# Sliding-window attention and dropless mixture of experts on one core: routing by pairs of batches, x stored times its probability, a tile's last additions moved into the next

## The chip, the cores and the metric

The kernel runs on one NeuronCore of a Trainium2 chip. The metric is device time in microseconds (us) of one execution: the median of the runs, 875.6 us before the change.

The engines are named as the profile names them: PE (TensorE matmuls; PEld its weight loads), DVE (VectorE), ACT (ScalarE), POOL (GpSimd) and SP (SyncE, which only issues DMAs here). Each works through its own queue in order and waits on semaphores for the others.

## The reference

```python
B, H, S, D = 8, 8, 576, 64            # attention: window of 64 positions, causal
mask = (rel >= 0) & (rel < 64)        # rel = query position - key position
attn = softmax(where(mask, q @ k.T / sqrt(D), -1e9));  o = attn @ v
x = o.transpose(0, 2, 1, 3).reshape(4608, 512)
logits = x @ w_gate                   # 8 experts
expert = argmax(logits);  gate = softmax(logits)[expert]
y[rows of expert e] = relu(x[rows of e] @ w1[e]) @ w2[e]   # w1: 512 x 1024, w2: 1024 x 512
out = gate[:, None] * y               # 4608 x 512, f32
```

Every token goes to one expert and none is dropped. With the inputs of this case the experts get 669, 400, 748, 505, 592, 390, 566 and 738 tokens.

## The kernel before, in words

**Attention.** Work goes by 16 units: a pair of batches (`bg`, 4 of them) times a pair of heads (`g`, 4). A unit has 9 blocks of 128 query rows and is worked in three steps of three blocks, so there are 48 steps. The loop at L381 writes a software pipeline: in step `s` it issues `scored(s+1)` (mask and scores into PSUM, row maximum L282 on DVE, exp L285 on ACT), `weighted(s-1)` (probabilities times values, L309; division into `xs`, L318), `turned(s+2)` (transposes of q and k, L233, copied out by ACT L238 and DVE L240), `flipped(s)` (transposes of the probabilities, L294, copied by DVE and ACT L296) and `x_turned(s-2)` (transposes of x, L332, copied at L335). A scheduler orders this stage's instructions by the order in the source and by readiness.

**Gate logits and the store of x.** `routed(u)` multiplies the turned x by the gate's weights (L355); after the fourth pair of heads the logits of the two batches are turned back and copied into the tile `logits` (L368). `x_turned` stores finished x rows into `x_dram` by DMAs on ACT's queue (L340, L346).

**Routing.** After all of attention, on the logits of all 4608 tokens at once (36 columns of 128 tokens, 8 experts), lines L420 to L540: the maximum and a one-hot of its first place (L448 to L454), the probability `gate` (L455 to L461), counts before each token by two f32 matmuls with a triangular and a full matrix of ones (L467, L468) and a scan (L470), how many tiles each expert takes (L480 to L497), the slot of each token (L505 to L512), and one-hots of the slot's low 7 bits (`lo`, L524) and of its column (`hi`, L526), the latter also times the token's number and its probability (L529, L530). 36 matmuls (L533) add these up into `slots`; `perm_i` (L537) says which token sits in each slot, `gate_t` (L539, L540) with which probability. The routing pool `rt` and the second weights' pool `wp` lie in memory that attention's pools had; `load_w` (L138, L139) fetches w1 and w2 of an expert on SP's queue.

**Experts.** Tiles of 256 tokens, in an order written out by hand (`manual_schedule`, L551). Each product of 2x2 blocks is done with seven block products instead of eight, so sums of blocks are formed: of the weights by POOL (`sums_w1`, `sums_w2`: four additions each, L121), of x and of the hidden layer by DVE (`sums_x`, and `left_sums` into `hs`, both L121 too). `body` is one tile: `hidden` (L609 to L631), `turn` (transposes of the next tile's x, L593, L594), `gather` (indirect DMA of x rows for the tile after that, L573), `output` (L640 to L671), `scatter` (indirect DMA of result rows to `out`, L582). In `output` every read of a product multiplies by the token's probability: ACT at L655, L656, L659, DVE at L647 (`onto`). A full tile has 256 tokens; an odd last chunk of 128 is done with plain matmuls (`plain_hidden`, `plain_output`). An expert runs its first tile inside `tc.If(chunks > 1)` (L735), then the odd one inside `tc.If(odd > 0)` (L740), then the others in nested Ifs (L743 to L751). The counts give 19 full tiles and 2 odd ones (experts 4 and 6). Where an If is not taken, every engine passes a block that raises its semaphore by what the skipped instructions would have, once its own earlier work is done.

**Order on POOL's and DVE's queues.** POOL: gather of the tile after next, scatter at the tile's end (behind DVE's last addition), the copy of the next probabilities, then `sums_w1(e+1)` ahead of an expert's first tile and `sums_w2(e+1)` behind it. DVE in `output`: four sums into `hs`, four of `sums_x`, then the seven `onto`.

Of the kernel before, what the change touches and what calls it, by code (L numbers as in the profile page):

```python
# [10 lines left out]
F32 = mybir.dt.float32  # L11
BF16 = mybir.dt.bfloat16
# [23 lines left out]
def kernel(  # L36
# [47 lines left out]
    logits = consts.tile([P, E, NJ], F32, name="logits")  # L84
    perm_i = consts.tile([P, NS], I32, name="perm_i")
    gate_t = consts.tile([P, NX, C + 1], F32, name="gate_t")
# [3 lines left out]
    starts_i = consts.tile([P, E], I32, name="starts_i")  # L90
    halves_i = consts.tile([P, E], I32, name="halves_i")
    w1v = moe_w1.rearrange("e (g p) f -> p e g f", p=P)
    w2v = moe_w2.rearrange("e (t p) d -> p e t d", p=P)
    weights = lambda pool, i: [
        pool.tile([P, 1, NG, FF], F32, name=f"w1_{i}"), pool.tile([P, 1, FT, DM], F32, name=f"w2_{i}")
    ]
    ws = [weights(consts, 0)]
# [3 lines left out]
    sums_of = lambda pool, i: (  # L101
        pool.tile([P, 4, HG, HD], F32, name=f"s1_{i}"), pool.tile([P, 4, HF, HM], F32, name=f"s2_{i}")
    )
    sums = [sums_of(consts, 0)]
# [18 lines left out]
    def w1q(e):  # L123
        w = ws[e % NW][0][:, 0]
        return [w[:, a * HG : (a + 1) * HG, f * HD : (f + 1) * HD] for f in range(2) for a in range(2)]

    def w2q(e):
        w = ws[e % NW][1][:, 0]
        return [w[:, f * HF : (f + 1) * HF, a * HM : (a + 1) * HM] for f in range(2) for a in range(2)]

    def sums_w1(e):
        form(left_sums(G, sums[e % NW][0], *w1q(e)))

    def sums_w2(e):
        form(right_sums(G, sums[e % NW][1], *w2q(e)))

    def load_w(e):
        nc.sync.dma_start(out=ws[e % NW][0][:], in_=w1v[:, e : e + 1, :, :])  # L138
        nc.sync.dma_start(out=ws[e % NW][1][:], in_=w2v[:, e : e + 1, :, :])  # L139
# [12 lines left out]
    with (  # L152
# [172 lines left out]
        def x_turned(s):  # L325
# [12 lines left out]
            if g == NG - 1 and c:  # L338
                x, t0 = xss[bg], (bg * BG + c - 1) * S
                nc.scalar.dma_start(  # L340
                    out=x_dram[t0 : t0 + SM, :].rearrange("(n p) d -> p n d", p=P), in_=x[:, (c - 1) * NV : c * NV, :]
                )
                if c == NST - 1:
                    for i in range(BG):
                        t0 = (bg * BG + i) * S + SM
                        nc.scalar.dma_start(out=x_dram[t0 : t0 + D, :], in_=x[i * D : (i + 1) * D, BG * NV, :])  # L346

        WC = 32
        def routed(u):

# [8 lines left out]
            if g == NG - 1:  # L359
# [3 lines left out]
                for m in range(ST):  # L363
# [3 lines left out]
                    )  # L367
                nc.vector.tensor_copy(  # L368
                    out=logits[:, :, bg * NTB : (bg + 1) * NTB].rearrange("p e (c m) -> p e c m", c=NST),
                    in_=tr[:, :, :, 0:E].rearrange("p m c e -> p e c m"),  # L370
                )

# [8 lines left out]
        for s in range(-2, N + 4):  # L381
            if s == N - 2 * NST:
                load_w(0)
            if s == N - NST:
                sums_w1(0)
                sums_w2(0)
# [16 lines left out]
    ws.append(weights(wp, 1))  # L403
    sums.append(sums_of(wp, 1))
    load_w(1)


    with (
# [3 lines left out]
        def iota(shape, pattern, base=0, cm=0):  # L412
            t = rt.tile(shape, F32, name=f"iota{len(iotas)}")
            nc.gpsimd.iota(
                t[:], pattern=pattern, base=base, channel_multiplier=cm, allow_small_or_imprecise_dtypes=True
            )
            iotas.append(t)
            return t

        iotas = []  # L420
        e_m = iota([P, E], [[1, E]], base=-E)
        lane = iota([P, P], [[1, P]])
        hi_id = iota([P, NS], [[1, NS]], base=-C)
        cuts = iota([P, NCUT], [[P, NCUT]])

        tok_m = rt.tile([P, NJ], F32, name="tok_m")
        tok_g = tok_m[:].rearrange("p (g j) -> p g j", j=NTB)
# [352 lines left out]
```

## Time and profile before

| | |
|---|---|
| time, median of 3 runs | 875.6 us (875.54 to 877.23) |
| the profiled execution | 876.49 us |
| its span, first to last instruction | 874.8 us |
| mean granted TensorE clock | 0.959 |
| PE busy | 780.4 us (89%) |
| PEld busy | 664.8 us (76%) |
| DVE busy | 430.0 us (49%) |
| ACT busy | 237.7 us (27%) |
| POOL busy | 307.7 us (35%) |
| HBM read, written | 73.94 MB, 20.45 MB |

Busy time is the time in which an engine had an instruction of the program at work. A row of a timeline gives the start in us, the length, the engine, the line, the operation, the tiles as out<-in, the shapes, and in square brackets the idle time before it with what ended it. A row of waits gives who waited for whom, the total in us, how often, and the longest. "DVEq" and "PEq" are an engine's sequencer, such as its branch at the line named. A window's row gives busy time and number of instructions of each engine, the granted clock, the share of the DMA engines and GB/s.

### The profile page before, as it was taken

The numbers are of one execution on the slowest core, as the hardware profiler recorded it, in microseconds if no ns is written. First come the engines' busy times: TensorE is split into PE (matmuls) and PEld (weight loads), VectorE is DVE, ScalarE is ACT, GpSimd is POOL, SyncE is SP. The second block draws the span as 40 slices with busy tenths as digits, with TensorE's granted clock in tenths as the row PEclk, the third lists the DMA queues.
The fourth block names the chain that finished last, engine by engine and source line by source line (L and its number), as shares of the span: only waits on it lengthen the run. The fifth ranks groups of instructions, "written<-read, shape, count | busy, mean of one in ns | idle before, by whom it ended". The sixth has DMA issues, their size and how long they took to land. (4 is left out here: it accounts for less than half of the span.)

```text
span 874.8 us, 17497 instructions
## 1 busy us (share of the span) xinstructions
PE 780.4 (89%) x6832; PEld 664.8 (76%) x6832; DVE 430.0 (49%) x818; ACT 237.7 (27%) x606; POOL 307.7 (35%) x312
## 2 busy tenths in 40 slices
PE   7998998998981479999998999889999899999992
PEld 5775776676750478999887999779888888888992
DVE  4664665665644543444436343545444436344341
ACT  4553554553530012222111221112122111121220
POOL 3221221245000063415626522735715626621121
PEclk9998999998995689999999999999999999999997
DMA  6668667878025011015143115115215143110110
GB/s 137 152 138 232 155 155 217 216 177 245 9 89 213 0 49 50 25 50 209 50 158 111 37 49 218 49 56 191 77 31 214 49 157 113 49 45 25 50 49 23
DMA packets 140302, 94.48 MB, mean 108 GB/s; under 512 B 118032, under 2 KB 118032, under 8 KB 140178
## 3 DMA queue, kind: packets, MB, share of 16 engines
q1 hardware_dynamic: 128274, 61.90, 25.3%
q0 software_dynamic: 7040, 21.50, 7.5%
q10 hardware_dynamic: 4864, 9.44, 3.0%
q8 instruction: 75, 1.23, 0.6%
q14 instruction: 49, 0.40, 0.2%
HBM read 73.94 MB, written 20.45 MB: 108 GB/s over the span
## 5 line engine op out<-in xcount | busy, mean ns | idle before, releaser
L609 PE MATMUL hp<-xs,s 128*128 128x128 f32 x912 | 108.4, 276 | 0.5 <-DVE part L618 0.5
L640 PE MATMUL yp<-s,hs 128*128 128x256 f32 x456 | 103.4, 381 | 4.7 <-DVE hs L121 4.7
L609 PEld LDWEIGHTS hp<-xs,s 128*128 128x128 f32 x912 | 105.3, 193 | 0.7 <-DVE part L618 0.7
L640 PEld LDWEIGHTS yp<-s,hs 128*128 128x128 f32 x456 | 85.9, 190 | 19.6 <-DVE hs L121 8.3
L582 POOL DMA_INDIRECT out_dram<-y,at_s x42 | 42.5, 1011 | 163.6 <-DVEq L745 51.4
L285 ACT ACTIVATE pr<-sc,mx 128x128 f32<-128x128 f32 x288 | 79.4, 374 | 70.6 <-DVE mx L282 52.6
L121 POOL TENSOR_TENSOR s<-w 128x1024 f32<-128x1024 f32 x32 | 78.3, 2449 | 57.2 <-DMA out_dram<-y,at_s 38.3
L609 PE MATMUL hp<-xq,w 128*128 128x128 f32 x608 | 76.6, 280 | 15.4 <-DVEq L740 7.9
L609 PEld LDWEIGHTS hp<-xq,w 128*128 128x128 f32 x608 | 73.0, 196 | 21.2 <-issue 21.0
L573 POOL DMA_INDIRECT xg<-x_dram,at_g x46 | 50.3, 1094 | 79.4 <-PE tp L593 69.1
L640 PE MATMUL yp<-w,hq 128*128 128x256 f32 x304 | 71.9, 379 | 0.0
L282 DVE TENSOR_REDUCE mx<-sc 128x3 f32<-128x384 f32 x96 | 49.1, 553 | 41.8 <-PE sc L275 40.3
L216 POOL COPY vb<-va 64x520 f32<-64x520 f32 x32 | 19.7, 616 | 126.7 <-DMA va<-in_v_dram 89.5
L647 DVE SCALAR_TENSOR_TENSOR party<-yp,gates,party 128x256 f32<-128x256 f32 x76 | 34.9, 479 | 57.4 <-PE yp L640 56.2
L640 PEld LDWEIGHTS yp<-w,hq 128*128 128x128 f32 x304 | 56.3, 190 | 6.8
L616 ACT COPY part<-hp 128x512 f32<-128x512 f32 x19 | 11.1, 585 | 160.5 <-PE hp L609 160.5
L121 DVE TENSOR_TENSOR hs<-hq 128x512 f32<-128x512 f32 x38 | 45.2, 1190 | 13.2 <-ACT hq L631 13.2
L618 DVE TENSOR_TENSOR part<-hp,part 128x512 f32<-128x512 f32 x19 | 13.1, 691 | 76.3 <-PE hp L609 76.3
L294 PEld LDWEIGHTS tr<-ident,pr 128*128 128x128 f32 x288 | 34.9, 146 | 20.0 <-ACT qT L238 8.3
L294 PE MATMUL tr<-ident,pr 128*128 128x128 f32 x288 | 49.7, 288 | 0.1
L275 PE MATMUL sc<-kT,qT 64*64 64x128 f32 x1152 | 47.2, 287 | 0.1
L275 PEld LDWEIGHTS sc<-kT,qT 64*64 64x64 f32 x1152 | 33.9, 138 | 12.6 <-issue 8.6
(141 smaller groups left out, 1350.9 us busy)
## 6 DMA issues: line engine op xcount, KB each, us to landing
w<-in_moe_w_dram SPq DMA_DIRECT2D x16, 2048.0 KB, 11.3
qs<-in_q_dram SPq DMA_DIRECT2D x64, 128.0 KB, 3.2
ks<-in_k_dram SPq DMA_DIRECT2D x64, 128.0 KB, 3.1
va<-in_v_dram SPq DMA_DIRECT2D x64, 128.0 KB, 2.8
x_dram<-xs ACTq DMA_DIRECT2D x8, 1024.0 KB, 6.1
qs<-in_q_dram SPq DMA_DIRECT2D x32, 32.0 KB, 2.6
ks<-in_k_dram SPq DMA_DIRECT2D x32, 32.0 KB, 2.2
vb<-in_v_dram SPq DMA_DIRECT2D x32, 32.0 KB, 2.7
```

What stands on the lines that cost most here:

```text
L121: op()
L216: nc.gpsimd.tensor_copy(out=vb[0:D, i].rearrange("p j h d -> p (j h d)"), in_=va[D:P, i].rearrange("p j h d -> p (j h d)"),)
L275: nc.tensor.matmul(out_, lhsT=qT[rows, t, a * WINDOW : (a + 1) * WINDOW], rhs=rhs, start=False, stop=True, skip_group_check=True,)
L282: nc.vector.tensor_reduce(out=mx[:], in_=scs[h][:], axis=AX.X, op=ALU.max, negate=True)
L285: nc.scalar.activation(out=pr[:, m, :], in_=scs[h][:, m, :], func=AF.Exp, bias=mx[:, m : m + 1])
L294: nc.tensor.transpose(out=tr[:, m, :], in_=prs[h][:, m, :], identity=ident[:])
L573: G.indirect_dma_start(out=xg[c][:], out_offset=None, in_=x_dram[:, :], in_offset=bass.IndirectOffsetOnAxis(ap=at_g[:, c : c + 1], axis=0),)
L582: put = G.indirect_dma_start(out=out[:, :], out_offset=bass.IndirectOffsetOnAxis(ap=at_s[:, c : c + 1], axis=0), in_=ys[c][:], in_offset=N ...
L609: nc.tensor.matmul(acc[:, f, :], lhsT=a[:, g, f * P : (f + 1) * P], rhs=b[:, g, :], start=(first and f == 0 and g == 0), stop=(g == HG - 1 ...
L618: V.tensor_tensor(out=u2[:], in0=y[:], in1=p1[:], op=ALU.add)
L640: nc.tensor.matmul(acc, lhsT=a[:, f, :], rhs=b[:, f, :], start=(first and f == 0), stop=(f == HF - 1), skip_group_check=True,)
L647: onto = lambda out, acc, c, more: V.scalar_tensor_tensor(out=out, in0=acc, scalar=gates[:, c : c + 1], in1=more, op0=ALU.mult, op1=ALU.add)
```

## The change

Three edits, with what goes along with them.

1. The routing is done for a pair of batches as soon as its logits are there, inside attention (`choose`): maximum, one-hot, probability, counts within the pair (9 columns) and a running `count`, the slot's high part `rkhi` and the one-hot `lo`. What needs all tokens stays behind attention: the experts' starts, the one-hot `hi` and the 36 matmuls, now in two halves. The one-hots, `lane`, `hi_id`, the matrices of ones and the token numbers (split into two parts, `tok_a` and `tok_b`) are bf16; their constants are built ahead of attention.
2. `store` multiplies x by its probability (ACT, DVE and POOL take every third column each) and then stores it. The experts compute on the scaled x; `gate_t`, `gates` and the scalings in `output` go.
3. The last three additions of a tile (`finish`) and its `scatter` move to the start of the next tile; after the last tile they are issued once more. `perm_i` of the tile before is used for that scatter, and the first tile scatters into rows out of bounds.

The weights are two tiles each now (`w1s`, `w2s`), and w2 and its sums of expert 0 lie in `wp`: `load_w2(0)`, `load_w1(1)` and `load_w2(1)` are issued after attention. `sums_w1(e+1)` moves behind the first tile of expert e and `sums_w2(e)` ahead of it.

```diff
-    def load_w(e):
-        nc.sync.dma_start(out=ws[e % NW][0][:], in_=w1v[:, e : e + 1, :, :])
-        nc.sync.dma_start(out=ws[e % NW][1][:], in_=w2v[:, e : e + 1, :, :])
+        form(right_sums(G, s2s[e % NW], *w2q(e)))
+    def load_w1(e):
+        nc.sync.dma_start(out=w1s[e % NW][:], in_=w1v[e])
+    def load_w2(e):
+        nc.sync.dma_start(out=w2s[e % NW][:], in_=w2v[e])
...
+    oh_all = consts.tile([P, E, NJ], BF16, name="oh_all")
+    rkhi = consts.tile([P, NJ], F32, name="rkhi")
+    lo = consts.tile([P, NJ, P], BF16, name="lo")
+    count = consts.tile([P, E], F32, name="count")
+    lane = consts.tile([P, P], BF16, name="lane")
...
+    iota = partial(G.iota, allow_small_or_imprecise_dtypes=True)
+    with tc.tile_pool(name="tmp", bufs=1) as tmp:
+        iota(e_m[:], pattern=[[1, E]], base=-E, channel_multiplier=0)
+        ids = tmp.tile([P, P], F32, name="ids")
+        iota(ids[:], pattern=[[1, P]], base=0, channel_multiplier=0)
+        V.tensor_copy(out=lane[:], in_=ids[:])
+        V.tensor_scalar_add(hi_id[:], ids[:, 0:NS], float(-C))
...
+        V.tensor_scalar(out=tok_i[:], in0=tok[:], scalar1=-1.0, scalar2=float(NT), op0=ALU.mult, op1=ALU.add)
+        V.tensor_single_scalar(low_i[:], tok_i[:], D - 1, op=ALU.bitwise_and)
+        V.tensor_copy(out=tok_b[:], in_=low_i[:])
+        V.tensor_tensor(out=tok_a[:], in0=tok_i[:], in1=low_i[:], op=ALU.subtract)
+        G.memset(ones[:], 1.0)
...
-            if g == NG - 1 and c:
-                x, t0 = xss[bg], (bg * BG + c - 1) * S
...
+                logits = small.tile([P, E, NTB], F32, name="logits")
...
+                store(bg, choose(bg, logits))
+        def choose(bg, logits):
+            js = slice(bg * NTB, (bg + 1) * NTB)
+            by_tok = lambda t: t.rearrange("p e j -> p j e")
+            new = lambda name, *shape, dt=F32: small.tile([P, *shape], dt, name=name)
+            mx = new("r_mx", NTB)
+            V.tensor_reduce(out=mx[:], in_=by_tok(logits[:]), axis=AX.X, op=ALU.max)
+            top = new("r_top", E, NTB)
+            V.tensor_tensor(out=top[:], in0=logits[:], in1=_ins(mx[:], 1, E), op=ALU.is_equal)
+            V.tensor_tensor(out=top[:], in0=top[:], in1=_inner(e_m[:], NTB), op=ALU.mult)
+            idx = new("r_idx", NTB)
+            V.tensor_reduce(out=idx[:], in_=by_tok(top[:]), axis=AX.X, op=ALU.min)
+            oh = oh_all[:, :, js]
+            V.tensor_tensor(out=oh, in0=_inner(e_m[:], NTB), in1=_ins(idx[:], 1, E), op=ALU.is_equal)
+            sums = ps_tr.tile([P, 2, E, NTB], F32, name="tr")
+            for i, w in enumerate((before, ones)):
+                nc.tensor.matmul(
+                    sums[:, i], lhsT=w[:], rhs=oh, start=(i == 0), stop=(i == 1), skip_group_check=True
+                )
+            pe = new("r_pe", E, NTB)
+            V.tensor_tensor(out=pe[:], in0=logits[:], in1=_ins(mx[:], 1, E), op=ALU.subtract)
+            nc.scalar.activation(out=pe[:], in_=pe[:], func=AF.Exp)
+            flat = lambda t: t.rearrange("p e j -> p (e j)")
+            inc = new("r_inc", E, NTB)
+            V.tensor_tensor_scan(
+                out=flat(inc[:]), data0=flat(keep[:]), data1=flat(sums[:, 1]), initial=0.0, op0=ALU.mult, op1=ALU.add
+            )
+            rank = new("r_rank", E, NTB)
+            V.tensor_tensor(out=rank[:], in0=inc[:], in1=_inner(count[:], NTB), op=ALU.add)
+            V.tensor_tensor(out=rank[:], in0=rank[:], in1=sums[:, 1], op=ALU.subtract)
+            V.tensor_tensor(out=rank[:], in0=rank[:], in1=sums[:, 0], op=ALU.add)
+            V.tensor_tensor(out=count[:], in0=count[:], in1=inc[:, :, NTB - 1], op=ALU.add)
+            V.tensor_tensor(out=rank[:], in0=rank[:], in1=oh, op=ALU.mult)
+            gate = new("gate", NTB)
+            V.tensor_reduce(out=gate[:], in_=by_tok(pe[:]), axis=AX.X, op=ALU.add)
+            V.tensor_scalar_add(gate[:], gate[:], 1e-9)
+            V.reciprocal(out=gate[:], in_=gate[:])
+            pos = new("r_pos", NTB, dt=I32)
+            with nc.allow_low_precision("integers"):
+                V.tensor_reduce(out=pos[:], in_=by_tok(rank[:]), axis=AX.X, op=ALU.add)
+            half = new("r_half", NTB, dt=I32)
+            V.tensor_single_scalar(half[:], pos[:], P.bit_length() - 1, op=ALU.arith_shift_right)
+            V.tensor_copy(out=rkhi[:, js], in_=half[:])
+            V.tensor_single_scalar(half[:], pos[:], P - 1, op=ALU.bitwise_and)
+            low = new("r_low", NTB, dt=BF16)
+            V.tensor_copy(out=low[:], in_=half[:])
+            V.tensor_tensor(out=lo[:, js], in0=_inner(low[:], P), in1=_ins(lane[:], 1, NTB), op=ALU.is_equal)
+            return gate
+        def store(bg, gate):
+            x = xss[bg]
+            for j in range(NTB):
+                y, s = x[:, j, :], gate[:, j : j + 1]
+                if j % 3 == 0:
+                    nc.scalar.activation(out=y, in_=y, func=AF.Copy, scale=s)
+                else:
+                    (V, G)[j % 3 - 1].tensor_scalar(out=y, in0=y, scalar1=s, scalar2=None, op0=ALU.mult)
+            for i in range(BG):
+                t0 = (bg * BG + i) * S
+                nc.scalar.dma_start(
+                    out=x_dram[t0 : t0 + SM, :].rearrange("(n p) d -> p n d", p=P), in_=x[:, i * NV : (i + 1) * NV, :]
+                )
+            for i in range(BG):
+                t0 = (bg * BG + i) * S + SM
+                nc.scalar.dma_start(out=x_dram[t0 : t0 + D, :], in_=x[i * D : (i + 1) * D, BG * NV, :])
...
             if s == N - 2 * NST:
-                load_w(0)
+                load_w1(0)
             if s == N - NST:
                 sums_w1(0)
-                sums_w2(0)
...
     wp = ctx.enter_context(tc.tile_pool(name="wp", bufs=1))
-    ws.append(weights(wp, 1))
-    sums.append(sums_of(wp, 1))
-    load_w(1)
+    s1s.append(s1_of(wp, 1))
+    w2s.append(w2_of(wp, 0))
+    s2s.append(s2_of(wp, 0))
+    w1s.append(w1_of(wp, 1))
+    w2s.append(w2_of(wp, 1))
+    s2s.append(s2_of(wp, 1))
+    load_w2(0)
+    load_w1(1)
+    load_w2(1)
...
+        new = lambda name, *shape, dt=F32: rt.tile([P, *shape], dt, name=name)
+        V.tensor_scalar_add(chunks_i[:], count[:], float(P - 1))
+        V.tensor_single_scalar(chunks_i[:], chunks_i[:], P.bit_length() - 1, op=ALU.arith_shift_right)
         V.tensor_single_scalar(odds_i[:], chunks_i[:], 1, op=ALU.bitwise_and)
         V.tensor_single_scalar(tiles_i[:], chunks_i[:], 1, op=ALU.arith_shift_right)
-        cum = rt.tile([P, E], F32, name="cum")
+        nt, cum, start = (new(n, E) for n in ("nt", "cum", "start"))
+        V.tensor_tensor(out=nt[:], in0=tiles_i[:], in1=odds_i[:], op=ALU.add)
         V.tensor_tensor_scan(out=cum[:], data0=ones[:, 0:E], data1=nt[:], initial=0.0, op0=ALU.mult, op1=ALU.add)
-        start = rt.tile([P, E], F32, name="start")
         V.tensor_tensor(out=start[:], in0=cum[:], in1=nt[:], op=ALU.subtract)
-        V.tensor_copy(out=starts_i[:], in_=start[:])
+        both = new("both", E)
+        V.scalar_tensor_tensor(
+            out=both[:], in0=start[:], scalar=float(C), in1=odds_i[:], op0=ALU.mult, op1=ALU.add
+        )
+        of = new("of", E, NJ)
+        V.tensor_tensor(out=of[:], in0=oh_all[:], in1=_inner(both[:], NJ), op=ALU.mult)
+        base, odd = new("base", NJ, dt=I32), new("odd", NJ, dt=I32)
+        with nc.allow_low_precision("integers"):
+            V.tensor_reduce(out=base[:], in_=of[:].rearrange("p e j -> p j e"), axis=AX.X, op=ALU.add)
+        V.tensor_single_scalar(odd[:], base[:], 1, op=ALU.bitwise_and)
+        early, at = new("early", NJ), new("at", NJ)
+        V.scalar_tensor_tensor(
+            out=early[:], in0=rkhi[:], scalar=float(C + 1), in1=odd[:], op0=ALU.is_lt, op1=ALU.mult
+        )
+        V.tensor_tensor(out=at[:], in0=rkhi[:], in1=base[:], op=ALU.add)
+        at_b = new("at_b", NJ, dt=BF16)
+        V.tensor_tensor(out=at_b[:], in0=at[:], in1=early[:], op=ALU.subtract)
+        hi = new("hi", NJ, NS, dt=BF16)
+        toks = new("toks", NJ, 2, NS, dt=BF16)
+        slots = ps_rt.tile([P, 2, NS], F32, name="slots")
+        for js in (slice(0, NJ // 2), slice(NJ // 2, NJ)):
+            n = NJ // 2
+            V.tensor_tensor(out=hi[:, js], in0=_inner(at_b[:, js], NS), in1=_ins(hi_id[:], 1, n), op=ALU.is_equal)
+            for i, v in enumerate((tok_a, tok_b)):
+                V.tensor_tensor(out=toks[:, js, i], in0=hi[:, js], in1=_inner(v[:, js], NS), op=ALU.mult)
+            for j in range(js.start, js.stop):
+                nc.tensor.matmul(
+                    slots[:].rearrange("p a s -> p (a s)"), lhsT=lo[:, j, :],
+                    rhs=toks[:, j].rearrange("p a s -> p (a s)"), start=(j == 0), stop=(j == NJ - 1),
+                )
+        perm = new("perm", NS)
+        V.tensor_scalar(out=perm[:], in0=slots[:, 0], scalar1=-1.0, scalar2=float(NT), op0=ALU.mult, op1=ALU.add)
+        V.tensor_tensor(out=perm_i[:], in0=perm[:], in1=slots[:, 1], op=ALU.subtract)
+        V.tensor_copy(out=starts_i[:, 0:E], in_=start[:])
+        V.tensor_copy(out=starts_i[:, E:], in_=cum[:, E - 1 : E])
...
+        V.tensor_tensor(out=halves_i[:], in0=halves_i[:], in1=starts_i[:, 0:E], op=ALU.add)
...
+        y1, v1, v2, v3 = (mp.tile([P, HM], F32, name=f"party{i}") for i in range(4))
...
+            product_y(yx, a11, b11)
+            nc.scalar.copy(out=y1[:], in_=yx)
+            product_y(yw, a22, t[:, 3])
+            product_y(yx, a12, b21, start=False)
+            nc.scalar.copy(out=ys[0][:, lo_], in_=yx)
             sums_x()
-            product(y, hs[:, 1], t[:, 1])
-            product(y2, hs[:, 2], t[:, 2])
-            onto(v2[:], y, 0, y1a[:])
-            onto(v3[:], y, 1, y1b[:])
-            onto(v3[:], y2, 1, v3[:])
-            product(w2, hs[:, 0], t[:, 0])
-            onto(ys[1][:, lo], w, 2, v3[:])
-            onto(ys[1][:, hi], w2, 1, v3[:])
-            onto(v2[:], w2, 0, v2[:])
-            product(x2, hs[:, 3], b22)
-            onto(ys[0][:, hi], x2, 0, v2[:])
+            product_y(yy, hs[:, 1], t[:, 1])
+            product_y(yy2, hs[:, 2], t[:, 2])
+            plus(v1[:], yy, y1[:])
+            plus(v3[:], yy2, v1[:])
+            product_y(yw2, hs[:, 0], t[:, 0])
+            V.tensor_tensor(out=ys[1][:, lo_], in0=v3[:], in1=yw, op=ALU.subtract)
+            product_y(yx2, hs[:, 3], b22)
+        def finish():
+            plus(v2[:], yw2, v1[:])
+            plus(ys[1][:, hi_], yw2, v3[:])
+            plus(ys[0][:, hi_], yx2, v2[:])
...
+            b11, b12, b21, b22 = w2q(e)
+            a11, a12 = hq[:, 0, 0], hq[:, 1, 0]
+            V.memset(v1[:], 0.0)
+            product_y(yx, a11, b11, stop=False)
+            product_y(yx, a12, b21, start=False)
+            nc.scalar.copy(out=ys[0][:, lo_], in_=yx)
+            product_y(yw2, a11, b12)
+            product_y(yx2, a12, b22)
...
+        def body(e, last, after, full):
+            finish()
+            scatter(last)
...
-            scatter(now)
-            G.tensor_copy(out=gates[:], in_=gate_t[:, nxt])
...
-                if e:
-                    load_w(e + 1)
-                sums_w1(e + 1)
+            if 0 < e < E - 1:
+                load_w1(e + 1)
+                load_w2(e + 1)
+            sums_w2(e)
...
+                return bass.ds(i * C, C), bass.ds((i + 3) * C, C)
...
             if e + 1 < E:
-                sums_w2(e + 1)
+                sums_w1(e + 1)
                 coming = counts(e + 1)
             with tc.If(odd > 0):
...
+        end = G.value_load(starts_i[0:1, E : E + 1], min_val=0, max_val=NTILE)
+        finish()
+        scatter(bass.ds(end * C, C))
```

## The prediction

> **What bounds the kernel now.** I read the stages first: busy time in four windows, cut at the end of attention, at the first expert matmul's transposes, at the last matmul and at the end.
>
> ```profile
> 0.00:261.00 261.00, 243.44 (x3228) 172.83 (x3228) 155.14 (x381) 129.93 (x405) 59.68 (x90) 0.97 0.64 159
> 261.00:311.40 50.40, 12.74 (x76) 11.47 (x76) 23.73 (x43) 0.44 (x1) 4.41 (x16) 0.62 0.29 109
> 311.40:858.70 547.30, 524.25 (x3528) 480.45 (x3528) 250.68 (x393) 107.35 (x200) 241.38 (x203) 0.99 0.25 86
> 858.70:874.80 16.10, 0.00 (x0) 0.00 (x0) 0.48 (x1) 0.00 (x0) 2.22 (x3) 0.66 0.08 31
> ```
>
> The columns are window, length, then PE, PEld, DVE, ACT, POOL busy, granted clock, DMA share, GB/s. Attention and the experts are PE's (93% and 96% busy); the 50 us of routing between them leave PE almost idle, and 16 us lie after the last matmul. So anything taken off the routing chain counts whole, anything added to DVE, ACT or POOL inside the other stages counts only where PE waits for it. Next the timeline of the routing.
>
> ```profile
> 260.46 0.23 DVE L368 COPY logits<-tr 128x72 f32<-128x72 f32 x1 [1.96 <-PE tr L364]
> 271.05 0.64 DVE L448 TENSOR_REDUCE r_mx<-logits 128x36 f32<-128x288 f32 x1 [10.36 <-DMA x_dram<-xs]
> 284.07 4.96 DVE L524 TENSOR_TENSOR lo<-half,iota 128x4608 f32<-128x4608 f32 x1
> 293.68 2.33 DVE L530 TENSOR_TENSOR hi<-hi,tok_m 128x2088 f32<-128x2088 f32 x1
> 296.07 10.49 PE L533 MATMUL slots<-hi,lo 128*128 128x116 f32 x72 [19.10 <-DVE hi L530]
> 306.60 0.22 DVE L537 TENSOR_SCALAR perm_i<-slots 128x58 int32<-128x58 f32 x1 [10.58 <-PE slots L533]
> ```
>
> 46 us in one chain: 10.4 waiting for the stores of x, 25 of DVE, 10.5 of one-hot matmuls. The wait is one for memory: r_mx is a routing tile, the routing pool takes the place of attention's pools, and it is released when the last reader there, the store of x, has landed. The third view is the first expert tile's timeline, where POOL forms weight sums beside DVE.
>
> ```profile
> 315.09 0.43 DVE L121 TENSOR_TENSOR xs<-xq,xs 128x256 f32<-128x256 f32 x1
> 315.44 3.12 DVE L121 TENSOR_TENSOR xs<-xq 128x256 f32<-128x256 f32 x1
> 315.90 2.36 POOL L121 TENSOR_TENSOR s<-w 128x1024 f32<-128x1024 f32 x1
> 343.58 1.69 PE L609 MATMUL hp<-xq,w 128*128 128x128 f32 x13 [1.50 <-DVEq L740]
> ```
>
> The same DVE subtraction takes 0.43 us alone and 3.12 beside a POOL sum: one waits until the other's whole instruction is over. The last row is the join after an expert's first tile, with the odd tile skipped: PE waits 1.50 us for DVE, which must finish the tile's last additions and pass the skipped block. The waits of the whole run add two rows:
>
> ```profile
> PE sc L254 <- ACT pr L285: 9.2, 7, 3.8
> PE yp L640 <- DVE hs L121: 4.7, 8, 0.8
> ```
>
> **The change, part by part.** The sum is made against the profiled execution (876.49 us; span 874.8, 1.7 outside it), 0.9 above the median of 875.6. About 0.2% (1.75 us) is what a measurement of this kernel can tell from no change.
>
> *Start.* Routing constants now come ahead of the mask on POOL and in scratch memory that the mask's pool reuses, so mask waits for the last DVE cast of them. The iotas and fills took 271.07 to 273.13 in the trace; with DVE's six small ops (0.2 each) mask starts about 3 us later, its last piece at some 9 instead of 5.9 us; PE first uses it at 7.26. Cost 1.0 us (0 to 2.5).
>
> *Choosing inside attention, three of four groups.* Each adds to DVE 12 ops of 72 elements (0.2, as L520's 0.20), 8 tiny ones (0.17), lo on 1152 elements (4.96/4 = 1.24), three scalings of 512 (0.4 to 0.5): about 6.3 us; to ACT an exp and three scalings, 2.1; to POOL three scalings near 0.6 (L216's copy of 520 takes 0.62); to PE two small matmuls. DVE is 59% busy here, a step of the pipeline lasts 5.4 us and leaves DVE about 2 idle, and PE already waits when the exp is late (9.2 us in all, at ACT's queued stores). A burst of 6.3 less 2 idle and 2 of buffered lead leaves 2.0 us a group: 6.0. Ends: 0 (cover holds) and 4.5 a group, 13.5 (nothing interleaves). The four stores of a group move behind the choosing, all on ACT's queue; the present stalls of 3.8, 1.7 and 2.5 us at them stay, I assume, since ACT's next exps still queue behind each issue.
>
> *Routing after the last logits (260.69).* Now serial: five DVE ops 1.25, PE 0.7 (the f32 pair of four times the columns took 2.3), scan to gate 2.4, four index ops and the reduce 1.1, lo 1.3, first scaling 0.5: store of x at +7.2 (it was issued at 255.00, before the logits). Landing after the first issue took 16.05 us (255.00 to 271.05) beside 4 MB of weights; the same again, since w2 of expert 0 and both of expert 1 are loaded into memory released by the choosing's own tiles: +23.3, 283.9. Only then may nt and what follows write: by tile sizes the weights' pool ends 128 bytes inside the small pool, so the routing pool still lies over x's. Chain: four tiny ops 0.84, of 0.50, reduce 0.67, four tiny 0.84, six builds of 1044 elements at 2.33/2088 each 7.0, the last 18 bf16 matmuls 1.8 (between a quarter of the f32 0.29 each, 1.3, and all of it, 5.2; nearest is L254's bf16 weight load, 0.10 each), latency 0.2, two ops 0.44: 12.3. perm_i at 296.2 against 306.8: −10.6 (−17 if x lands in 10 us, −6 if in 20).
>
> [...] No run here shows bf16 builds yet.
>
> *Experts: order on POOL.* The scatter moves from a tile's end into the next tile, and the sums of w1 for the next expert follow the first tile directly. POOL's gather ends 16.6 us after a tile's start (832.80 to 849.38). Today the sums run at 405.7, before that gather, and hold up hs (PE's 4.7 us in eight waits); or they run during hidden, where DVE reads PSUM and L618 keeps its 0.69 beside them. In the change four sums follow at 849.4 and DVE's four sums_x were due at 849.65: each subtraction waits for one POOL op, four periods of 2.36+0.4, so the last ends near 860.9; v1, v3 and the first half of y1 queue behind them: 862.2. PE ends its tile at 858.65. Where the odd tile is skipped, PE's next matmul waits for DVE to pass the skip, 0.75 later (342.65 to 343.41): PE resumes at 863.05, a gap of 4.4 for today's 1.4. Five joins (342.1, 422.1, 477.4, 558.8, 684.0): 7.1 becomes 22, +14.9. With the odd tile taken (experts 4 and 6) 7 us of plain matmuls cover it. The hs waits vanish: −4.6. Sums of w2 start after a skipped block's DMA waits, past sums_x: nothing. Ends for the five joins: −4.7 (DVE never late) and +18 (one period more).
>
> [...]
>
> *Last additions moved.* At joins between experts PE's own branches take 0.75 of the 0.82 (394.84), so −0.8 over eight. The additions themselves (three of 0.48) lie beside the next tile's first products, 1.9 us each, and come before u2 is due; uncovered they would cost 1.4 a tile. One addition and two scaled copies less per tile are off the path.
>
> *End.* Three additions and a register load stand ahead of the final scatter (+1.0), but POOL passes its skipped blocks (862.6 to 866.2) before it and not after: −4. Sum −3 (−4 to +1).
>
> Sum: 1.0 + 6.0 − 10.6 + 14.9 − 4.6 − 0.8 − 3.0 = +2.9; 879.4 for the profiled kind, 878.5 against the median.
>
> **Rivals.** *Faster: DVE gets ahead of the sums.* The order at 849.4 against 849.65 is a quarter of a microsecond. If one sums_x is served first, the chain ends a period (2.7) sooner, +1.4 over five joins; if two or more are, the joins shrink to branch time, −4.7. Totals 865 and 859, 862 between. Against it: at 315.44 DVE was held although POOL's row starts later. It decides from POOL's sums starting 0.3 us later. Chance 0.22. *Attention hides the choosing:* it fills DVE's idle 41%; 7 us less, 872. Chance 0.17. For it: interleaving with ready work. *Slower, attention pays:* the bursts stop PE from the point where DVE's backlog exceeds one pipeline step's lead (2 us); at 4.5 a group +7.5: 886. For it, nine microseconds of such stalls already. Chance 0.16. [...]
>
> **How the numbers follow.** Forecast 878.5, chance 0.42, own range 874 to 884; 0.03 is left for others. Slower: 0.34 of the forecast's, all 0.16, 0.02 elsewhere: 0.52. Faster: 0.20 of the first rival's, 0.11 of the second's, 0.02 of the forecast's, 0.02 elsewhere: 0.35. Within: 0.13. The range 860 to 888 reaches over both rivals; below it lie fast landings of x together with free joins, above it both bad ends.
>
> **What would show it.** Right: DVE's sums_x near 2.7 us in each expert's first tile, PE gaps near 4 us with DVE's skip as releaser at five joins, no more hs waits, nt waiting for x's store, perm_i near 303 (later by attention's 7). Wrong: sums_x at 0.42 everywhere, the routing chain not waiting for x, or PE's attention time up by over 12 us.

## The result and the profile after

The changed kernel takes 884.88 us (median of 4 runs, 881.17 to 886.64) against 875.57 (4 runs): ratio 1.010, 95% interval 1.0061 to 1.0139. It is slower by about 1%, a loss beyond the 0.2% that can be told from no change, on the side that the prediction gave 0.52, inside its range and 6.4 us above its likeliest time. That it came so near is in part luck: attention lies 13.0 us above its term and routing 7.4 below. The profiled execution took 885.91 us, its span is 884.1 (before: 874.8).

Stage by stage, from the two traces (us; "first product" is the first expert matmul):

| | before | after | difference | predicted |
|---|---|---|---|---|
| attention, to the last copy of the logits | 260.46 | 280.44 | +20.0 | +7.0 |
| routing, from there to the end of `perm_i` | 46.35 | 28.31 | -18.0 | -10.6 |
| to the first product | 6.96 | 7.07 | +0.1 | 0 |
| experts, to the end of the last product | 544.88 | 555.67 | +10.8 | +9.5 |
| behind the last product | 16.13 | 12.64 | -3.5 | -3.0 |
| span | 874.8 | 884.1 | +9.3 | +2.9 |

The windows of the changed kernel, cut at the same events (columns as before: window, length, PE, PEld, DVE, ACT, POOL busy, granted clock, DMA share, GB/s):

```profile
0.00:280.70 280.70, 251.84 (x3234) 175.19 (x3234) 177.43 (x460) 136.78 (x417) 67.77 (x105) 0.93 0.56 136
280.70:313.60 32.90, 4.04 (x38) 3.56 (x39) 20.75 (x56) 2.21 (x4) 7.50 (x6) 0.53 0.78 273
313.60:871.50 557.90, 531.38 (x3560) 497.15 (x3560) 262.04 (x383) 95.87 (x181) 243.55 (x190) 0.97 0.25 84
871.50:884.10 12.60, 0.00 (x0) 0.00 (x0) 1.08 (x3) 0.00 (x0) 2.02 (x2) 0.70 0.11 39
```

Attention's window holds 6 more matmuls than before, yet PE is busy 251.8 us and not 243.4, at a clock of 0.93 and not 0.97: of the 20 us, 8.4 are busy time at a lower clock and the rest is waiting. Where, the timeline of the first group shows:

```profile
83.02 0.21 PE L425 MATMUL tr<-oh_all,before 128*128 128x72 bf16 x1 [1.38 <-DVE oh_all L421]
85.55 0.90 PE L372 MATMUL tr<-ident,xs 128*128 128x128 f32 x3 [1.43 <-DVE r_rank L440]
85.85 2.32 ACTq L470 DMA_DIRECT2D x_dram<-xs  x2
95.44 1.16 ACTq L475 DMA_DIRECT2D x_dram<-xs  x2
96.64 0.48 ACT L336 COPY pT<-tr 128x384 f32<-128x384 f32 x1 [10.58 <-issue]
97.17 0.37 PE L349 MATMUL px<-vb,pT 128*64 128x65 f32 x1 [4.65 <-ACT pT L336]
```

PE first waits twice for DVE's choosing: at its own count matmuls, and at the transposes of x, whose PSUM buffer the counts hold until DVE has read them. Then ACT issues the two large stores and stands at the small ones from 88 to 95.4; its copy of pT is queued behind them, and PE waits 4.65 us for that. In the second group ACT's idle time before that copy is put down to a load of k, 9.9 us long. By the semaphores in the trace, a small store waits in both groups until a load on SP's queue that uses the same semaphore has landed; the store is issued within 0.1 us of that. In the third group it waits for POOL's last scaling instead, 1.1 us. In windows the clock shows what follows:

```profile
82.00:84.00 2.00, 0.98 (x9) 0.76 (x9) 2.00 (x10) 1.43 (x6) 0.00 (x0) 1.00 0.49 111
84.00:86.00 2.00, 0.57 (x3) 0.46 (x3) 2.00 (x6) 2.00 (x4) 1.96 (x2) 0.64 0.75 170
92.00:98.00 6.00, 1.35 (x19) 0.95 (x19) 0.00 (x0) 1.36 (x4) 0.00 (x0) 0.50 1.17 306
100.00:102.00 2.00, 2.00 (x43) 1.67 (x39) 0.89 (x2) 0.38 (x3) 0.00 (x0) 0.59 0.44 94
102.00:104.00 2.00, 2.00 (x21) 1.36 (x16) 1.79 (x6) 1.75 (x7) 1.13 (x2) 1.00 0.62 141
```

From 84.6 to 101.6 PE runs at half clock. The three groups cost 7.0, 9.4 and 2.5 us more than the same steps before (by how far the row maxima L322 shift against before over each), although those steps held stalls of 3.8, 1.7 and 2.5 us already.

The timeline of the routing answers to the one of before:

```profile
280.44 0.23 DVE L401 COPY logits<-tr 128x72 f32<-128x72 f32 x1 [1.96 <-PE tr L396]
284.65 2.07 ACTq L470 DMA_DIRECT2D x_dram<-xs  x2
287.89 1.91 ACTq L475 DMA_DIRECT2D x_dram<-xs  x2
289.42 0.37 SPq L136 DMA_DIRECT2D w<-in_moe_w_dram  x1
296.62 0.17 DVE L528 TENSOR_TENSOR nt<-tiles_i,odds_i 128x8 f32<-128x8 int32 x1 [7.33 <-DMA x_dram<-xs]
301.58 1.24 DVE L559 TENSOR_TENSOR toks<-hi,tok_a 128x1044 bf16<-128x1044 bf16 x1
306.34 1.90 PE L561 MATMUL slots<-toks,lo 128*128 128x116 bf16 x18 [0.26 <-DVE toks L559]
308.53 0.22 DVE L567 TENSOR_TENSOR perm_i<-perm,slots 128x58 int32<-128x58 f32 x1
```

`nt` waits for x to land, as predicted; the chain behind it takes 12.1 us (12.3 predicted). The store starts 4.0 us after the copy of the logits has ended (7.2 predicted), as DVE and ACT scale x ahead of the index operations and of `lo`, and it has landed 12.0 us later (16 predicted). The weight loads start behind it, at 289.42, which is the likely reason: in rt_low below they start ahead of it, and the landing takes 17.2.

The end of the first expert's first tile, with POOL's sums beside it:

```profile
335.53 3.28 DVE L116 TENSOR_TENSOR hs<-hq,hs 128x512 f32<-128x512 f32 x1
335.87 2.38 POOL L116 TENSOR_TENSOR s<-w 128x1024 f32<-128x1024 f32 x1
338.32 2.69 POOL L116 TENSOR_TENSOR s<-s,w 128x1024 f32<-128x1024 f32 x1
338.73 2.57 DVE L116 TENSOR_TENSOR xs<-xq 128x256 f32<-128x256 f32 x1
340.98 2.53 POOL L116 TENSOR_TENSOR s<-w 128x1024 f32<-128x1024 f32 x1
341.33 2.46 DVE L116 TENSOR_TENSOR xs<-xq,xs 128x256 f32<-128x256 f32 x1
343.47 2.52 POOL L116 TENSOR_TENSOR s<-w,s 128x1024 f32<-128x1024 f32 x1
343.71 2.56 DVE L116 TENSOR_TENSOR xs<-xq 128x256 f32<-128x256 f32 x1
346.20 0.41 DVE L116 TENSOR_TENSOR xs<-xs,xq 128x256 f32<-128x256 f32 x1
348.90 1.41 PE L639 MATMUL hp<-xq,w 128*128 128x128 f32 x5 [3.77 <-DVEq L769]
```

Four of DVE's instructions in a row end only when one of POOL's has ended, and PE resumes 3.77 us late. The waits of the run count five of these:

```profile
PE hp L639 <- DVEq L769: 18.5, 5, 3.8
```

### The profile page after: what moved, and what is told of

Read it like the earlier page. It is cut to its first block, busy times and chain, and to the rows that moved or that the text cites. A ratio compares the mean times of both kernels' runs of the same rounds, so it can differ in the third digit from the quotient of the medians.

```text
span 884.1 us, 17543 instructions
## 1 busy us (share of the span) xinstructions
PE 787.3 (89%) x6832; PEld 675.9 (76%) x6832; DVE 461.3 (52%) x902; ACT 234.9 (27%) x602; POOL 320.8 (36%) x303
## 5 line engine op out<-in xcount | busy, mean ns | idle before, releaser
L639 PE MATMUL hp<-xs,s 128*128 128x128 f32 x912 | 110.9, 279 | 1.4 <-DVE part L648 1.4
L639 PEld LDWEIGHTS hp<-xs,s 128*128 128x128 f32 x912 | 108.0, 197 | 1.6 <-DVE part L648 1.6
L639 PE MATMUL hp<-xq,w 128*128 128x128 f32 x608 | 84.6, 299 | 24.9 <-DVEq L769 18.5
L639 PEld LDWEIGHTS hp<-xq,w 128*128 128x128 f32 x608 | 80.5, 213 | 30.0 <-issue 29.7
L671 PE MATMUL yp<-w,hq 128*128 128x256 f32 x368 | 86.0, 379 | 0.0
L671 PEld LDWEIGHTS yp<-w,hq 128*128 128x128 f32 x368 | 68.3, 190 | 8.4
L322 DVE TENSOR_REDUCE mx<-sc 128x3 f32<-128x384 f32 x96 | 49.4, 552 | 38.2 <-PE sc L315 37.3
L667 DVE TENSOR_TENSOR party<-yp,party 128x256 f32<-128x256 f32 x60 | 25.3, 422 | 74.3 <-PE yp L671 54.4
L116 DVE TENSOR_TENSOR xs<-xq 128x256 f32<-128x256 f32 x44 | 51.2, 1164 | 12.4 <-ACT xq L626 12.4
L349 PE MATMUL px<-vb,pT 128*64 128x65 f32 x512 | 42.7, 235 | 9.9 <-ACT pT L336 8.9
L349 PEld LDWEIGHTS px<-vb,pT 128*64 128x64 f32 x512 | 34.9, 147 | 17.5 <-ACT pT L336 9.6
## 6 DMA issues: line engine op xcount, KB each, us to landing
w<-in_moe_w_dram SPq DMA_DIRECT2D x16, 2048.0 KB, 10.5
```

Source lines behind the costliest of these rows:

```text
L116: op()
L322: nc.vector.tensor_reduce(out=mx[:], in_=scs[h][:], axis=AX.X, op=ALU.max, negate=True)
L349: nc.tensor.matmul(px[a * D : (a + 1) * D, h, m, :], lhsT=pTs[h][:, m, a * D : (a + 1) * D], rhs=vt[:, h, :], start=True, stop=True, skip_ ...
L639: nc.tensor.matmul(acc[:, f, :], lhsT=a[:, g, f * P : (f + 1) * P], rhs=b[:, g, :], start=(first and f == 0 and g == 0), stop=(g == HG - 1 ...
L667: plus = lambda out, a, b: V.tensor_tensor(out=out, in0=a, in1=b, op=ALU.add)
L671: nc.tensor.matmul(acc, lhsT=a[:, f, :], rhs=b[:, f, :], start=(start and f == 0), stop=(stop and f == HF - 1), skip_group_check=True,)
```

## The experiments

Medians are of 4 runs or more, ratios to the kernel before on the same chip. The stages of the profiled execution of each:

| kernel | median | ratio (95%) | attention | routing | experts | end |
|---|---|---|---|---|---|---|
| late_sums | 860.21 | 0.983 (0.9807 to 0.9853) | 277.9 | 27.9 | 530.7 | 12.6 |
| tail_back | 917.26 | 1.048 (1.0455 to 1.0504) | 281.9 | 28.0 | 586.3 | 15.7 |
| order_back | 877.86 | 1.0025 (1.0003 to 1.0047) | 279.6 | 28.3 | 544.4 | 15.8 |
| store_sp | 859.36 | 0.9831 (0.9801 to 0.9861) | 260.5 | 24.8 | 549.6 | 12.6 |
| before_sp | 851.29 | 0.9738 (0.9708 to 0.9768) | 243.4 | 38.5 | 544.4 | 16.1 |
| rt_low | 881.23 | 1.0072 (1.0044 to 1.01) | 281.1 | 23.8 | 553.6 | 12.6 |
| both | 835.99 | 0.9564 (0.9535 to 0.9593) | 262.3 | 24.7 | 526.9 | 12.6 |
| both_low | 834.79 | 0.9556 (0.9524 to 0.9588) | 262.0 | 20.6 | 529.0 | 12.7 |
| keep_clock | 902.87 | 1.0326 (1.0295 to 1.0358) | 283.2 | 27.9 | 573.4 | 12.6 |
| all4 | 824.35 | 0.9426 (0.9389 to 0.9463) | 254.3 | 20.6 | 527.2 | 12.6 |

**late_sums: the sums get out of DVE's way.**

```diff
             if e + 1 < E:
-                sums_w1(e + 1)
                 coming = counts(e + 1)
             with tc.If(odd > 0):
...
+            if e + 1 < E:
+                sums_w1(e + 1)
             with tc.If(chunks > 3):
```

> The changed kernel with the sums of w1 of the next expert moved from directly behind an expert's first tile to behind the odd tile's If, so that they follow the skipped block on POOL and start after DVE's sums_x. Lock theory (the sums on POOL hold DVE's sums_x for a whole instruction each, 2.5 us, and so make PE wait 3.7 us at five joins): sums_x back near 0.42 us, the five gaps 1.0 to 1.4 us, total 872 to 874. Rival (the gap comes from the moved additions and the skipped block, whatever POOL does): gaps stay at 3.7 us and the time at 885.

The experts take 24.9 us less than in the changed kernel, twice what was expected. The timeline shows the cause that was named: with POOL starting 1.5 us after the end of DVE's last subtraction, each takes 0.42 us, and PE's gap at the join is 0.43.

```profile
334.69 0.42 DVE L116 TENSOR_TENSOR xs<-xq 128x256 f32<-128x256 f32 x1
335.14 0.43 DVE L116 TENSOR_TENSOR xs<-xq,xs 128x256 f32<-128x256 f32 x1
335.82 0.42 DVE L116 TENSOR_TENSOR xs<-xs,xq 128x256 f32<-128x256 f32 x1
337.78 2.34 POOL L116 TENSOR_TENSOR s<-w 128x1024 f32<-128x1024 f32 x1 [3.36 <-DMA xg<-x_dram,at_g]
344.12 1.58 PE L639 MATMUL hp<-xq,w 128*128 128x128 f32 x12 [0.43 <-PEq L768]
```

The second half of the gain lies elsewhere: the five tiles that hold a join fall by 14.8 us together, and the five behind them by 10.1 (28.1, 28.2, 27.2, 29.5 and 28.0 become 25.5, 26.6, 25.5, 26.6 and 26.5). The windows of the first 6 us behind the joins say why. In the changed kernel, at three of the five:

```profile
348.90:354.90 6.00, 6.00 (x31) 6.00 (x32) 1.09 (x3) 0.59 (x1) 2.21 (x3) 0.56 0.24 90
432.81:438.80 5.99, 5.99 (x39) 5.99 (x40) 1.57 (x4) 0.59 (x1) 2.22 (x3) 0.72 0.23 88
573.47:579.50 6.03, 6.03 (x28) 6.03 (x29) 1.09 (x3) 0.59 (x1) 2.22 (x3) 0.50 0.23 87
```

and behind the first join of late_sums:

```profile
344.10:350.10 6.00, 5.98 (x53) 6.00 (x54) 1.50 (x4) 0.88 (x2) 5.41 (x6) 1.00 0.13 46
```

31 matmuls at a clock of 0.56 in the one, 53 at full clock in the other.

**keep_clock: the wait is filled, not shortened.** 12 matmuls without use stand behind each expert's first tile.

```diff
                 body(e, *place(at), True)
+            for i in range(12):
+                nc.tensor.matmul(hps[2][:, 0:2, :], lhsT=ident[:], rhs=xq[:, 0, 0], ...)
```

> The changed kernel with 12 matmuls (128x256, into a free product buffer, result unused) on PE behind an expert's first tile, 2.8 us of work in which PE would wait for DVE. Theory (the granted clock falls to half when PE has idled some 3 us, and the next tile starts at half clock for 5 to 6 us, 2.6 us lost at each of the five joins): the joins stay as late as they are, the tiles behind them fall from 28 to 29.4 us to about 25.6 to 26.5, total 872 to 875. Rival (the tiles behind the joins are slow for another reason, such as POOL's transfers of that time): 885 to 888.

The total was a miss: each of these f32 matmuls is two records, and a new one starts every 0.22 us, so the filling took 5.3 us and not 2.8, more than the wait, and it ran in all eight experts. The part that tells the theories apart came out as the clock theory (the wait lowers the clock, and the tile behind it pays) has it: the five tiles behind the joins take 25.5, 26.6, 25.5, 26.5 and 26.5 us, as in late_sums, and the clock stays at 1.00 although DVE is held by POOL as in the changed kernel. A timeline of the first join, and a window behind it:

```profile
345.91 2.53 POOL L116 TENSOR_TENSOR s<-w,s 128x1024 f32<-128x1024 f32 x1
346.15 2.56 DVE L116 TENSOR_TENSOR xs<-xq 128x256 f32<-128x256 f32 x1
347.41 5.34 PE L767 MATMUL hp<-xq,ident 128*128 128x256 f32 x24
```
```profile
353.20:359.20 6.00, 6.00 (x54) 6.00 (x55) 1.46 (x4) 0.91 (x2) 2.21 (x3) 1.00 0.24 90
```

**tail_back and order_back: the third edit undone, alone and with its order.**

```diff
-            finish()
-            scatter(last)
             (hidden if full else plain_hidden)(e)
...
+            finish()
+            scatter(now)
```

> The changed kernel with the third edit undone: the last three additions and the scatter stand at a tile's end again, the sums stay where the change put them. Lock theory: the scatter, which waits for DVE's last addition, is again ahead of the sums on POOL, so sums_x run free and the five gaps fall to about 1.4 us (-11.5); the end grows by 3 to 3.5 us as POOL passes its skipped blocks after the last scatter: 876 to 878. Rival (moving the additions has nothing to do with the gaps): gaps stay at 3.7 us, 888.

The five gaps did fall to 1.4 us, but the kernel became 32 us slower, which neither theory held. The timeline of the second expert's first tile:

```profile
408.97 2.36 POOL L116 TENSOR_TENSOR s<-w 128x1024 f32<-128x1024 f32 x1 [7.38 <-DMA out_dram<-y,at_s]
```
```profile
419.31 1.22 PE L671 MATMUL yp<-s,hq 128*128 128x256 f32 x2 [5.21 <-POOL s L116]
```

With the scatter at the tile's end, POOL passes the skipped blocks only when it has landed, 7.4 us later; `sums_w2(e)`, which the change had put ahead of the tile that needs it, comes too late, and PE waits 4.7 to 6.5 us in six experts. The scatter's place and the sums' places belong together. So order_back undid both:

```diff
-            sums_w2(e)
+            if e == 0:
+                sums_w2(0)
+            if e + 1 < E:
+                sums_w1(e + 1)
...
-                sums_w1(e + 1)
+                sums_w2(e + 1)
                 coming = counts(e + 1)
```

> The changed kernel with the whole third edit undone, order of the weight sums too: additions and scatter at a tile's end, sums of w1(e+1) ahead of the first tile of expert e, sums of w2(e+1) behind it, as before the change. It leaves the routing by pairs and the scaled x alone. If the experts' loss is all in the third edit's order: experts near the 545 us of before, tail near 16, total 876 to 878, so that attention's +20 and routing's -18 nearly cancel. If the scaled x or the missing scalings carry part of it: experts off 545 by more than 4 us.

Experts 544.4 (before 544.9), end 15.8, total 877.86, as the first of the two theories has it: all of the experts' loss is in the third edit and its order, and what is left of the change, the scaled x with it, costs the experts nothing on balance. The first two edits alone cost 0.25%: +19 us in attention, -18 in routing.

**store_sp and before_sp: no engine that computes stands at a store.** In both, the four `nc.scalar.dma_start` of x become `nc.sync.dma_start`, in the changed kernel and in the one before.

> The changed kernel with the four stores of x of a group issued on SP's queue and not on ACT's. Theory A (ACT stands at the stores behind loads in flight, its pT copies behind it, and PE waits 4.7 and 4.3 us for them in the first two groups, with the clock at half for longer): these waits go, attention ends 8 to 12 us earlier, total 873 to 877. Theory B (the chain of DVE's choosing sets the cost of a group): attention ends less than 3 us earlier, 882 to 885. SP's loads queue behind the stores; if they come late, PE waits for q and k instead.

> The kernel before with its four stores of x per pair of batches on SP's queue and nothing else changed. It prices what the choosing inside attention costs once no engine that computes stands at a store. If the choosing is hidden (rival of the prediction), attention ends here at about 258 to 260 us, as in store_sp (260.5). If the choosing has a price of its own, the stalls of 3.8, 1.7 and 2.5 us go and attention ends near 247 us, so that choosing costs some 13 us, 4.4 a group; total then about 862, against 876 if nothing moves.

Attention ends 20.0 us earlier in store_sp, at 260.5: theory A, and more than it asked. But that is not because the choosing is free. The kernel before gains 17.0 us by the same move (3.8, 1.7 and 2.5 us of stalls, and the half clock behind them), and ends attention at 243.4, where 247 was expected; PE is busy there 234.6 us and not 243.4. The window of the first stores, before and in before_sp:

```profile
78.00:90.00 12.00, 7.95 (x77) 5.50 (x73) 3.75 (x11) 2.85 (x9) 1.86 (x4) 0.72 0.83 187
78.00:90.00 12.00, 12.00 (x149) 8.17 (x149) 8.34 (x22) 7.54 (x25) 2.25 (x4) 1.00 0.70 208
```

So the choosing costs 17.0 us where no store is in the way, 5.6, 6.4 and 5.3 us for the three groups by the times between the copies of the logits. The waits for DVE stay in store_sp:

```profile
82.58 0.21 PE L425 MATMUL tr<-oh_all,before 128*128 128x72 bf16 x1 [1.38 <-DVE oh_all L421]
85.10 0.55 PE L372 MATMUL tr<-ident,xs 128*128 128x128 f32 x3 [1.43 <-DVE r_rank L440]
```

With the 0.3 to 0.7 us that follow they make 3.1 to 3.5 us a group; the rest of the 5.7 goes with the half clock behind them (0.58 and 0.57 from 86 to 90). Set beside before_sp, store_sp pays 17.0 us in attention for 13.7 less in routing (24.8 against 38.5): with the stores out of ACT's way too, the routing by pairs, issued in one burst, is a loss of 3.3 us.

**rt_low: routing's tiles off x's memory.** `s1` and `s2` of the second expert move from `wp` into a pool opened after routing.

> The changed kernel with two tiles of weight sums of the second expert (s1, s2) allocated after routing, so that routing's tiles lie over memory of attention that is free early and not over x's. Theory (nt waits 7.3 us only for the memory of the x being stored): nt no longer waits for the store, perm_i 7 us earlier, total 878; the weight loads may start ahead of the x stores and slow them, but x must have landed only when the first gather starts. Rival (the landing of x binds anyway, through the gather): perm_i earlier, first expert matmul at the same place, 884 to 885.

`nt` no longer waits and routing is 4.5 us shorter, not 7: the weight loads, whose memory is now free at 276.3, go ahead of x's stores, and the clearing of the experts' tiles, now ahead of `perm_i` in DVE's queue, waits for x until 302.5, 17.2 us after the first issue and not 12. So the edit took away one wait and made the landing later, and it does not price the wait alone.

**both, both_low and all4: do the parts add up?**

> The changed kernel with both moves: sums of w1 behind the odd tile's If, and the stores of x on SP's queue. If the two losses lie in different stages and add up (24.7 and 25.5 us): 834 to 837. If one hides part of the other: above 842.

> As both, with routing's tiles over memory that is free early. Here the weight loads stand behind the stores on SP's queue and cannot slow them. If nt's wait for the store (4.1 us in store_sp) is on the chain: 4 us faster than both, 830 to 833. If the landing of x binds through the cleared tiles and the gather: no difference.

The two losses add up: 48.9 us against 24.7 and 25.5. Routing's tiles bring `perm_i` 4.3 us earlier, of which 2.2 are lost in the first tile; the medians differ by 1.2 us, less than the runs can tell apart. all4 spreads the choosing of the first three groups over the following steps (one-hot; a step later the two count matmuls; then the low part; scaling and each store in steps of their own).

> As both_low, with the choosing of the first three groups spread over the pipeline's next steps: one-hot in one step, the two count matmuls a step later, the slot's low part another step later, scaling and each store in steps of their own. It differs from both_low in that alone. If the choosing's 17 us in attention (260.5 against 243.4 us) are PE waiting for a chain that is issued in one burst and the half clock after it: attention ends at 247 to 251 us, total 820 to 824. If they are work that DVE has no room for: attention stays near 261, total 834.

824.35 us, 5.7% below the kernel before and the fastest version here. Attention ends at 254.3: 7.7 us came back against both_low, between the two forecasts, and 10.9 remain over before_sp, for 18.0 less in routing (4.1 of them from routing's tiles): here the routing by pairs pays. The first group costs 0.9 us more than in before_sp and the third 2.6, but the second 7.7; there PE waited 1.72 us for ACT's exps and 1.66 for a division of DVE's, queued with the choosing. Whether another order would take those away was not tried.

## Why the prediction was right and wrong, point by point

- **Attention, the step that failed.** "A burst of 6.3 less 2 idle and 2 of buffered lead leaves 2.0 us a group: 6.0", upper end 13.5. Measured: 19.7 us. The sum counted DVE's work and its cover, and left out two things. First, PE has a place of its own in the choosing: two count matmuls in PE's queue that wait for the one-hot, and a PSUM buffer held until the counts are read (3.1 to 3.5 us a group in store_sp). Second, the clock: a stall was priced at its length, and with the half clock behind it, it cost twice that here (8 us of stalls, 17 us by before_sp). The cover was also read too large: in the steps from 90 to 140 of before, 4.8 us each, DVE is busy 68% and has 1.6 us left, not 2. That the present stalls stay was half right: two grew to 4.7 and 4.3 us, the third went. The stores' move to SP's queue takes 20.0 us out of the changed kernel and 17.0 out of the one before, so the stores make 3.0 of attention's 20 and the choosing 17. POOL's scalings, taken as near 0.6 us, are 1.6 to 1.8 each, and in the third group and behind the last logits the small stores wait for the last of them.
- **Start.** +1.0 predicted, +0.3 measured from the fourth step on.
- **Routing.** -10.6 predicted, -18.0 measured; the text's own other end was "−17 if x lands in 10 us". The mechanism held, with `nt` waiting for x's memory; two terms were mis-sized. The store started 3.2 us sooner than the sum has it, and it landed in 12.0 us and not 16: the 16 were taken from a row in which 4 MB of weights went beside it, and here they came behind. The bf16 terms were right: that the builds cost as much an element as in f32 was the author's estimate, which no run had shown, and they took 1.24 us for 1044 elements against 2.33 for 2088 in f32, so nothing saved on DVE; 18 matmuls took 1.90 against 1.8. The "quarter of the f32" at the low end of that last term is shown by no run; the 18 took 0.106 us each.
- **Joins.** +14.9 predicted for gaps of 4.4; they were 3.7 (+11.4), as the first of POOL's four periods fell on `hs`. What the row of 3.12 us told of a subtraction beside one of POOL's sums, the runs show again: 2.46 to 2.57 us beside POOL, 0.42 without, in the same line. Unpriced were the slow tiles behind the joins. Against late_sums, the order of the sums costs 24.9 us, 14.8 in the joins and 10.1 behind them.
- **The rest of the third edit.** -5.4 predicted (hs waits and joins between experts; the latter, 0.07 us at each of eight, make 0.6 and not the 0.8 of the sum). What +10.8 leaves behind +11.4 for the joins and +10.1 for the tiles behind them is -10.7: 7.7 are PE's waits that are gone, the hs waits (4.7) and those for gathered x (2.0) among them; the other 3.0 were not followed to their rows. So the experts' sum came out at +9.5 for +10.8 by luck: the slow tiles were missing, and this gain and the joins were off the other way. In late_sums the experts lie 14.1 us under before, as the five gaps fall to 0.42 or 0.43 us there, near the 0.5 that the sum's lower end of -4.7 implies.
- **End.** -3.0 predicted, -3.5 measured.
- **Rivals.** "DVE gets ahead of the sums" (859 to 865) did not happen in this kernel, but late_sums makes it happen and takes 860. "Attention hides the choosing" is refuted by before_sp, "attention pays" (886) came true beyond its 4.5 us a group; it had 0.16.
- **Its own signs.** Of those for being right, the held sums_x (2.5 us), the five gaps behind DVE's skip (3.7), the end of the hs waits and `nt`'s wait for x came true; so did one of those for being wrong, attention up by over 12 us.

## What to carry to other kernels

Work moved under a busy engine's stage is not priced by the free share of the engine that does it: follow each instruction that it puts into the other queues, the bound engine's first, and ask what waits in front of it and behind it. A stall of PE can cost its length and the clock afterwards (8.0 us of stalls at the stores of the kernel before cost it 17.0); read the granted clock in windows of 2 us around each stall before pricing what a new one costs. Keep DMA issues that may wait off the queues that compute, and move an engine's long instructions past the short ones that they hold up (DVE's subtractions took 0.42 us alone and 2.5 beside POOL's sums): the second of these was worth 24.7 us here and the first 25.5, each more than the whole change.

## What the runs showed of the hardware

- The granted clock fell to 0.50 after several short waits: 1.38, 1.43 and 0.67 us, with 1.1 and 0.6 us of matmuls between them (store_sp, first group), or 1.71 and 0.45 us (before, at 144). Single gaps of 1.4 and 2.5 us (before, at 342 and 587) left it at 1.00. Gaps of 3.7 us lowered it at all five joins of the changed kernel, but in other runs with the same gaps not at each: behind two joins of rt_low (3.75 and 3.65 us) and one of store_sp (3.66) it stayed at 1.00, and the tiles there took 25.5, 25.5 and 26.6 us as in late_sums. So the length of one gap does not decide alone. At the five joins of the changed kernel the fall came 2.3, 3.6, 4.0, 2.9 and 3.4 us after PE's last matmul ahead of the gap had ended, at the third 0.4 us after PE had resumed; no run shows the "some 3 us" of keep_clock's theory as a limit. In the clock records of the changed kernel's attention and joins every spell at 0.50 lasts 3.4 us or a multiple of it, up to 17.1. In the 3.4 us ahead of the first of them (81.15 to 84.56) PE was busy for 1.58 us.
- Once down, the clock stayed there while PE worked in pieces: about 17 us in the first group, with PE busy for 10.5 of them, 3 to 6 us behind a join where PE was fully busy.
- A DMA issue on ACT's queue waited up to 7 us for a load issued on SP's queue. 2 MB of x were on the DMA engines at the time (share 1.17 from 92 to 98), and that load, issued at 87.8, landed at 95.4, where the median of such loads is 3.1 us: the stores, it seems, delayed what they waited for. That order of cause was not tested by itself.
